# Attention, mixture of experts and a dense layer on one core: routing steps moved to another place on VectorE, an output tile put into the values' bank, and the end of the attention laid out anew

## Chip, core and metric

The kernel runs on one core of one Trainium2 chip. The metric is the device time in microseconds of one execution. Before the change it is 894.07 us, the median of 3 runs (893.64 to 894.19).

## What is computed

The reference chains three layers, all in float32:

```python
scores = q @ k.T / sqrt(64) + cum[:, None] - cum[None, :]   # cum: running sum of log f; causal
attn   = softmax(scores) @ v                                # 4 batches x 8 heads x 576 x 64
x      = attn, heads side by side                           # 2304 tokens x 512
logits = x @ w_gate + modality_bias[modality_id]            # 8 experts
e      = argmax(logits);  gate = softmax(logits)[e]
x      = gate * (relu(x @ w1[e]) @ w2[e])                   # w1: 512 x 1024, w2: 1024 x 512
h      = x @ w_in;  out = max(0.01 * h, h) @ w_out          # 512 -> 2048 -> 512
```

## The kernel before

**Attention (0 to 208 us).** Two heads make a group `g`; there are 16 groups, four to a batch. Each group goes through `first` (scores of query blocks 0 and 1), `last` (scores of block 4), `third` (block 2) and `fourth` (block 3). In these functions the group before is finished at the same time: `tr` transposes its probabilities on PE into PSUM tiles `pt_c`, ACT copies them to `tt`, `pv` multiplies them with the values in two parts (`pv_0`, `pv_1`, written to the one buffer of the pool `psv`), DVE copies the parts to `xu` and `xub`, and `xout` multiplies each with the identity beside the gate's weights (`xo_0`, `xo_1`). From `xo` DVE reads four times: `x` and `lp` of either part. `pt` and `xo` tiles rotate through the buffers of one pool, `pst`, so a transpose can be written only when DVE has read an `xo` tile of some time before. DVE also takes the maxima of the scores (`nm`) and prepares the operands of later groups (`raw`, `aq`).

**Routing.** `route(b)` is a generator of small steps for batch `b`: logits, the maximum `mx`, the one-hot `oh` of the chosen expert, ranks `rk` by matmul, and in the last step `lall`, five comparisons on DVE. `route1` makes the table of the first four expert slots by a matmul `tp` over `lall`, computes the row numbers from it on POOL and gathers the tokens of slots 0 and 1 (`xg`). Steps alternate between DVE, POOL, ACT and PE. `routed()` takes the next step of the oldest generator, whatever it is; it is called at fixed places of a group, and so a step lands where the count falls:

```python
        def routed(n=1):
            for _ in range(n):
                if routing and next(routing[0], 1):
                    routing.pop(0)
```

**Drain (208 to 224 us).** After the last group its tail remains: two `pt` tiles, `pv` and `xo`. The work of `drain` is put between that of slot 0's first matmul: `trx` transposes the gathered tokens (`tx`), `part0(k)` splits block `k` of the weights into a high part (ACT, `w1h`) and a low part (DVE, `w1l`), and starts the load of slot 1's weights. `gemm1` then makes `h` from three products a block, `keep` applies the activation on ACT (`hs`).

**Expert slots (to 470 us).** Slots of up to 128 tokens of one expert follow (`step`). Slots 1 to 3 split their weights only where the expert is another than that of the slot before: ACT and DVE read the word `nb` and branch (`tc.If` in `split`). In these inputs the branches aren't taken. The last batch's routing goes on in these steps; its places are the table `side`, as are those of `finish`, which makes the table of all further slots.

**Dense layer (480 to 890 us).** It is bound by PE and is not touched.

Work of each engine goes out in the order in which the code issues it; within some stretches (`ordered`) a scheduler keeps the order only for the engines that are named.

Of the kernel before, what the change touches and what calls it, by code (L numbers as in the profile page):

```python
# [74 lines left out]
def fused(ctx: ExitStack, tc, qk0, qk2, vp, f, mid, wg, mb, w1, w2, w_in, w_out, out):  # L75
# [93 lines left out]

    def parts(which, k):  # L170
        raw, hi, lo = (w2r, WL["2h"], WL["2l"]) if which else (w1r, w1h, WL["1l"])
        nc.scalar.copy(hi[k], raw[k])  # L172
        nc.vector.tensor_tensor(lo[k], raw[k], hi[k].bitcast(F32), ALU.subtract)  # L173
# [25 lines left out]
    with tc.tile_pool(name="pst", bufs=PST, space=PSUM) as pst:  # L199
# [277 lines left out]
        def pv(g, part):  # L477
            vt = vts[g]
            w = (XA, XB)[part]
            pv_ = psv.tile([P, 512], F32, tag="v", name=f"pv{g}_{part}")  # L480
            blocks = [(0, 0), (1, P), (2, 2 * P)] if part == 0 else [(0, 0), (1, 0), (2, 0), (3, 0), (4, P)]
            sb = st.pop((g, part))
            for b, q0 in blocks:
                for j in range(2):
                    nc.tensor.matmul(pv_[64 * j:64 * j + 64, q0:w], lhsT=vt[:, j, b, :], rhs=sb[:, j, b, q0:w], start=(b == 0), stop=(b == blocks[-1][0]))
            if part == 0:
                xu = a2.tile([P, w], F32, tag="xu", name=f"xu{g}")
            else:
                xu = xub
            st[g, "x", part] = xu  # L490
            nc.vector.tensor_copy(xu[:, :w], pv_[:, :w])

        def xout(g):
# [10 lines left out]
            for part, c0, n in ((0, 0, 3), (1, 3, 2)):  # L504
                xu = st.pop((g, "x", part))
                ps = pst.tile([P, 512], F32, tag="t", name=f"xo{g}_{part}")
                for i in range(n):
                    nc.tensor.matmul(ps[:, i * HW:(i + 1) * HW], lhsT=xu[:, i * P:(i + 1) * P], rhs=idw[:, gg, :], start=True, stop=True)
                i0 = ps[:, :n * HW].rearrange("p (c d) -> p c d", d=HW)
                sc = rr[:, c0:c0 + n, :].unsqueeze(3)  # L510
                for o, a, w in ((x[:, c0:c0 + n, gg * P:(gg + 1) * P], slice(0, P), D), (lp[:, c0:c0 + n, gg, :], slice(P, HW), E)):
                    nc.vector.tensor_tensor(o.rearrange("p c (j d) -> p c j d", j=2), i0[:, :, a].rearrange("p c (j d) -> p c j d", j=2), sc.to_broadcast([P, n, 2, w]), ALU.mult)
            if gg == H // 2 - 1:
                routing.append(route(b))
                if b == B - 1:
                    t0 = b * S
                    nc.sync.dma_start(xs[t0:t0 + 4 * P, :DM].rearrange("(c p) d -> p c d", p=P), x[:, 0:4, :DM])
                    nc.sync.dma_start(xs[t0 + 4 * P:t0 + S, :DM], x[:64, 4, :DM])
                if b == B - 2:
                    routing.append(route1(pre, (B - 1) * NC))  # L520
# [4 lines left out]

        RP = [pst, "t"]
# [22 lines left out]
        def route(b):  # L549
# [31 lines left out]
            rk = RP[0].tile([P, 512], F32, tag=RP[1], name=f"rk{b}")  # L581
            nc.tensor.matmul(rk[:, 0:4 * E], lhsT=before, rhs=oh[:, 0:4, :], start=True, stop=False)
            nc.tensor.matmul(rk[:, 4 * E:5 * E], lhsT=before[:64, :], rhs=oh[:64, 4, :], start=False, stop=False)
            nc.tensor.matmul(rk[:, 5 * E:6 * E], lhsT=onesb[:64, :], rhs=oh[:64, 4, :], start=False, stop=False)
            for c in range(4):
                nn = NC - c
                nc.tensor.matmul(rk[:, (c + 1) * E:6 * E].rearrange("p (c e) -> p c e", e=E), lhsT=onesb, rhs=oh[:, c, :].unsqueeze(1).to_broadcast([P, nn, E]), start=False, stop=(c == 3))
# [3 lines left out]
            if b < B - 1:  # L591
                nc.vector.reciprocal(x[:, :, DM], gs)
                for c in ((0, 2), (2, 4), (4, 5)) if b < B - 2 else ((0, 4), (4, 5)):
                    stores.append((b, x, *c))
            else:
                nc.vector.reciprocal(gs, gs)
                t0 = b * S
                nc.sync.dma_start(xs[t0:t0 + 4 * P, DM:].rearrange("(c p) d -> p c d", p=P), gs[:, 0:4].unsqueeze(2))
                nc.sync.dma_start(xs[t0 + 4 * P:t0 + S, DM:], gs[:64, 4:5])
# [11 lines left out]
            yield  # L611
            for c in range(NC):
                r = rows_of(c)
                nc.vector.tensor_scalar(lall[:r, b * NC + c, :], col[:r], pq[:r, c:c + 1], None, ALU.is_equal)

# [11 lines left out]
        def scan(a, n):  # L627
            t = [rt.tile([P, 4 + E], F32, name=f"scan{n}{i}") for i in range(2)]
            for i in t:
                nc.gpsimd.memset(i, 0.0)  # L630
            nc.gpsimd.tensor_copy(t[0][:, 4:], a)
            for s in (1, 2, 4):
                nc.gpsimd.tensor_add(t[1][:, 4:], t[0][:, 4:], t[0][:, 4 - s:4 + E - s])
                t = t[::-1]
            inc = t[0][:, 4:]
            exc = rt.tile([P, E], F32, name=f"exc{n}")
            nc.gpsimd.tensor_sub(exc, inc, a)
            return inc, exc
# [44 lines left out]
        def route1(tp, m):  # L683
# [9 lines left out]
            yield  # L693
# [19 lines left out]
            yield  # L713
            next(tb)
            yield
# [8 lines left out]
        routing = []  # L724

        def routed(n=1):
            for _ in range(n):
                if routing and next(routing[0], 1):
                    routing.pop(0)


        def first(g):
# [4 lines left out]
            store(1 + (g > 12))  # L737
            routed()
            if g == NG - 1:
                for w in range(2):  # L740
                    for k in range(4):
                        wload(0, w, k)
            for c in cs:
                c()
            for _ in then or ():
                pass

        def last(g):
            then = qk4(g) if g < NG else None
            if g:  # L750
                tr(g - 1, 4, (0, 1))
                routed()
# [4 lines left out]
        def third(g):  # L757
            then = qk(g, 2) if g < NG else None
            if g:
                routed()  # L760
# [7 lines left out]
        def fourth(g):  # L768
# [10 lines left out]
            routed()  # L779
# [5 lines left out]
        def finish_routes():  # L785
            while routing:
                if next(routing[0], 1):
                    routing.pop(0)
# [20 lines left out]
        def part0(k):  # L809
            parts(0, k)  # L810
            wload(1, 0, k)

        with ordered(tc, MS):
            prep_hi(1)
            for g in range(NG):
# [15 lines left out]
                if g:  # L831
# [3 lines left out]
                    routed()  # L835
                third(g)
                if not g:
                    last(g)
                fourth(g)
                routed()  # L840
# [86 lines left out]
    with tc.tile_pool(name="rt2", reuse_waits="tile", bufs=1) as rt2, \  # L927
# [17 lines left out]
        def split(t, which, k):  # L945
            if not 0 < t < K1:
                parts(which, k)
                if t + 1 < NS:
                    wload(t + 1, which, k)
            elif k == 3:  # L950

                if not WD:
                    WD.append(nc.values_load(nb[0:1, 0:1], engines=(mybir.EngineType.Activation, mybir.EngineType.DVE), min_val=0, max_val=2 ** K1 - 1))
                with tc.If(((WD[0] >> t) & 1) != 0):
                    for i in range(4):
                        parts(which, i)
                for i in range(4):
                    wload(t + 1, which, i)

        WD = []  # L960
# [54 lines left out]
        def step(t):  # L1015
            nx = t + 1 < NS
            if not t:
                split(t, 1, 0)
                split(t, 1, 1)
            keepg(t)  # L1020
            if t == K1 - 1:
                next(fini)
            if t + 2 < NS and t + 2 != K1:
# [3 lines left out]
            aside(t, "load")  # L1027
            if 0 < t < TE:
# [21 lines left out]
            if nx:  # L1050
# [22 lines left out]
        def finish():  # L1073
# [6 lines left out]
            tiles_of(nsl, cnt, P - 1)  # L1080
            nc.gpsimd.tensor_sub(nsl, nsl, used)
            inc, exc = scan(nsl, 2)
            nc.gpsimd.tensor_scalar(nt, inc[:, E - 1:E], float(K1), None, ALU.add)
            nc.gpsimd.tensor_sub(exc, exc, used)
# [49 lines left out]
        RP[:] = pmx, "tx"  # L1134
        fini = finish()
        late = routing.pop(0)
        for k, w in (((0, "b"), late), ((0, "d"), late), ((0, "d"), late), ((1, "load"), late), ((1, "a1"), late), ((1, "b"), fini), ((1, "pool"), late), ((1, "d"), late), ((1, "d"), fini), ((2, "load"), fini), ((2, "b"), fini)):
# [150 lines left out]
```

## Time and profile before

| what | value |
|---|---|
| median of 3 runs | 894.07 us (893.64 to 894.19) |
| profiled execution, its time | 891.73 us |
| profiled execution, its span | 890.0 us |
| TensorE clock granted, mean over the span | 0.991 of full speed |
| PE busy | 854.0 us, 96% of the span |

The span is that from the first to the last instruction of the profiled execution; its time is 1.7 us longer. The profiled execution is 2.3 us below the median of the three timed runs. All rows of the trace are of this one execution. A releaser named behind `<-` in a row is the instruction whose semaphore came last; `ACTq` and `DVEq` are the engines' sequencers, which run branches and loads of registers.

### The profile page before, as it was taken

The page shows a single profiled execution, that of the slowest core. Times are in us where ns is not written, and L with a number is a line of the kernel's source. Part 1 is how long each engine was busy: PE and PEld are TensorE (multiplying, and loading weights), DVE is VectorE, ACT ScalarE, POOL GpSimd, SP SyncE. Part 2 cuts the span into 40 slices and gives each one's busy share as a digit, 9 for nine tenths or more (in the row PEclk, how much of TensorE's full clock was granted, in tenths as well). Part 3 has the DMA queues.
Part 4 walks back from the last instruction along what each step waited for, and adds up shares of the span by engine and source line. Part 5 has one row for each costly group of instructions (what it writes and reads, how often), then busy time and mean ns, then how long its engine had stood idle before and what let it go on. Part 6 is the DMA issues. An engine that isn't in the chain of part 4 may idle for free. (4 is left out here: it accounts for less than half of the span.)

```text
span 890.0 us, 14390 instructions
## 1 busy us (share of the span) xinstructions
PE 854.0 (96%) x4733; PEld 707.6 (80%) x4733; DVE 583.8 (66%) x952; ACT 505.6 (57%) x969; POOL 194.3 (22%) x342
## 2 busy tenths in 40 slices
PE   5999999998899999999999999999999999999996
PEld 3788778886678888888787788888888888888885
DVE  6677677774558999999985373387337943473333
ACT  5787777875348999999984353453223422242221
POOL 5003122251737344544441000000000000001112
PEclk9999999999999999999999999999999999999998
DMA  5776776775268245121322240032001300011111
GB/s 152 206 183 190 207 206 179 201 178 198 78 205 301 69 153 168 55 70 41 115 96 60 64 143 13 1 99 91 0 1 48 119 25 0 1 48 48 48 48 72
DMA packets 33604, 92.93 MB, mean 104 GB/s; under 512 B 7957, under 2 KB 8629, under 8 KB 33522
## 3 DMA queue, kind: packets, MB, share of 16 engines
q1 hardware_dynamic: 28690, 76.70, 29.9%
q0 software_dynamic: 4800, 15.23, 5.0%
q8 instruction: 39, 0.64, 0.3%
q14 instruction: 43, 0.35, 0.1%
q10 hardware_dynamic: 32, 0.01, 0.0%
HBM read 132.09 MB, written 14.99 MB: 165 GB/s over the span
## 5 line engine op out<-in xcount | busy, mean ns | idle before, releaser
L1180 ACT COPY us<-u 128x512 f32<-128x512 f32 (+1 forms) x80 | 43.5, 544 | 163.7 <-PE u L1178 163.6
L1181 DVE SCALAR_TENSOR_TENSOR us<-u,us 128x512 f32<-128x512 f32 (+1 forms) x80 | 51.0, 637 | 125.8 <-ACT us L1180 125.2
L1178 PE MATMUL u<-fxl,whii 128*128 128x512 f32 (+1 forms) x320 | 118.1, 369 | 0.0
L1178 PE MATMUL u<-fxh,wloi 128*128 128x512 f32 (+1 forms) x320 | 117.9, 369 | 0.0
L1178 PE MATMUL u<-fxh,whii 128*128 128x512 f32 (+1 forms) x320 | 116.9, 369 | 0.7 <-ACT fxh L878 0.7
L1198 PE MATMUL a<-whio,gh 128*128 128x512 f32 x280 | 109.7, 392 | 0.0
L1198 PE MATMUL a<-wloo,gh 128*128 128x512 f32 x280 | 109.2, 390 | 0.0
L1198 PE MATMUL a<-whio,gl 128*128 128x512 f32 x280 | 103.2, 390 | 0.0
L173 DVE TENSOR_TENSOR w1l<-w1r,w1h 128x1024 fp32r<-128x1024 f32 x72 | 87.0, 1226 | 11.7 <-ACT w1h L172 11.4
L1208 POOL DMA_INDIRECT out<-acc,tid x18 | 17.7, 983 | 326.4 <-DVE acc L1205 272.0
L173 DVE TENSOR_TENSOR w2l<-w2r,w2h 128x1024 fp32r<-128x1024 f32 x68 | 80.7, 1227 | 1.2 <-ACT w2h L172 1.0
L399 ACT ACTIVATE p<-sc,nm 128x128 f32<-128x128 f32 (+3 forms) x128 | 66.0, 524 | 25.2 <-DVE nm L394 23.0
L1183 ACT CAST gh<-us 128x512 fp32r<-128x512 f32 (+1 forms) x76 | 44.6, 587 | 57.8 <-DVE us L1181 38.1
L172 ACT CAST w1h<-w1r 128x1024 fp32r<-128x1024 f32 x72 | 73.8, 1053 | 1.6 <-PE h L190 1.5
L1184 DVE TENSOR_TENSOR gl<-us,gh 128x512 fp32r<-128x512 f32 (+1 forms) x76 | 49.3, 648 | 38.3 <-ACT gh L1183 37.4
L394 DVE TENSOR_REDUCE nm<-sc 128x2 f32<-128x256 f32 (+1 forms) x64 | 51.0, 818 | 30.1 <-PE sc L390 26.6
L172 ACT CAST w2h<-w2r 128x1024 fp32r<-128x1024 f32 x68 | 69.3, 1050 | 2.4 <-PE y L983 1.3
L1178 PEld LDWEIGHTS u<-fxh,whii 128*128 128x128 f32 x320 | 60.2, 188 | 11.1 <-ACT fxh L878 0.9
L1178 PEld LDWEIGHTS u<-fxl,whii 128*128 128x128 f32 x320 | 60.3, 188 | 10.3
L1178 PEld LDWEIGHTS u<-fxh,wloi 128*128 128x128 f32 x320 | 60.3, 188 | 10.3
L983 PE MATMUL y<-w2h,hh 128*128 128x512 f32 x160 | 65.0, 406 | 0.0
L983 PE MATMUL y<-w2h,hl 128*128 128x512 f32 x160 | 62.9, 393 | 0.0
(296 smaller groups left out, 1858.4 us busy)
## 6 DMA issues: line engine op xcount, KB each, us to landing
w1r<-w SPq DMA_DIRECT2D x88, 512.0 KB
w2r<-w SPq DMA_DIRECT2D x82, 512.0 KB
rwi<-w_in SPq DMA_DIRECT2D x16, 512.0 KB
rwo<-w_out SPq DMA_DIRECT2D x16, 512.0 KB
raw<-qk SPq DMA_DIRECT2D x14, 576.0 KB
vt<-vp SPq DMA_DIRECT2D x16, 320.0 KB
xr<-yd SPq DMA_DIRECT2D x18, 256.5 KB
bk<-aq SPq DMA_DIRECT2D x15, 288.0 KB
```

Source lines behind the costliest of these rows:

```text
L172: nc.scalar.copy(hi[k], raw[k])
L173: nc.vector.tensor_tensor(lo[k], raw[k], hi[k].bitcast(F32), ALU.subtract)
L394: nc.vector.tensor_reduce(nm, view, axis=AX.X, op=ALU.max, negate=True)
L399: st["exp"] = nc.scalar.activation(pt[:, j, :], view[:, j, :], AF.Exp, bias=nm[:, j:j + 1], scale=1.0, accum_out=sms[g % 3][:, c, j:j + 1])
L983: nc.tensor.matmul(Yp[t], lhsT=ap[:, k * P:(k + 1) * P], rhs=wp[k // 2][:, k % 2, :], start=(k == 0 and i == 0), stop=(k == NFB - 1 and i ...
L1178: nc.tensor.matmul(ps, lhsT=w[:, c], rhs=x[:, k, :], start=(k == 0 and i == 0), stop=(k == NKB - 1 and i == 2))
L1180: nc.scalar.copy(us, ps)
L1181: nc.vector.scalar_tensor_tensor(us, ps, 0.01, us, ALU.mult, ALU.max)
L1183: nc.scalar.copy(gh, us)
L1184: nc.vector.tensor_sub(gl, us, gh.bitcast(F32))
L1198: nc.tensor.matmul(A[b][i], lhsT=x[:, c], rhs=w, start=(first and m == 0), stop=(last and m == 2))
L1208: d = nc.gpsimd.indirect_dma_start(out=out[:, :], out_offset=bass.IndirectOffsetOnAxis(ap=tid[:, c:c + 1], axis=0), in_=Y[b, i], in_offset ...
```

## The change

Four things change.

1. Routing steps have named places. A table `plan` maps a place in a group (`first`, `last`, `third`, `idle`, `end`, `after`) to the batch whose next step goes there. The place `idle` is new: it stands between the copy `xub` and the maximum of block 3's scores. One small multiplication (`eq` with `rev`) goes from POOL to DVE.
2. For groups up to 13, `xo_1` has no tile of `pst` any more. It is written to columns 192 to 479 of the bank in which `pv_1` of the same group stood in columns 0 to 191.
3. `drain` is written in another order, and `part0` is taken apart into `high` (ACT) and `low` (DVE). `high(0, 0)` goes up into the last group. The loads of slot 1's weights stand together behind the splits.
4. The branch of slot 1 (`split(1, 0, 3)`) is issued directly after `keep(0)`. The last batch has a generator of its own, `late_route`, wholly on DVE except for its matmul and its exponential; `side` has other places for it and for `finish`, whose scan moves from POOL to DVE. The fourth slot's table matmul is issued after `gemm1` of slot 3 has begun, and its gather behind that.

```diff
+                st[g, "half"] = pv_
...
-                ps = pst.tile([P, 512], F32, tag="t", name=f"xo{g}_{part}")
+                ps = st.pop((g, "half"))[:, XB:] if part and g < NG - 2 else pst.tile([P, 512], F32, tag="t", name=f"xo{g}_{part}")
...
-                routing.append(route(b))
+                routing[b] = (route if b < B - 1 else late_route)(b)
...
-            nc.gpsimd.tensor_tensor(eq, eq, rev.unsqueeze(1).to_broadcast(shp), ALU.mult)
-            yield
+            nc.vector.tensor_tensor(eq, eq, rev.unsqueeze(1).to_broadcast(shp), ALU.mult)
...
+        def late_route(b):
...
+            mx, eq, m2, lm = t1("mx"), t3("eq"), t1("m2"), t3("lm")
+            nc.vector.tensor_reduce(L, lp, axis=AX.X, op=ALU.add)
+            nc.vector.tensor_add(L, L, bia[:, b * NC:(b + 1) * NC])
+            nc.vector.tensor_reduce(mx, L, axis=AX.X, op=ALU.max)
+            nc.vector.tensor_tensor(eq, L, mx.unsqueeze(2).to_broadcast(shp), ALU.is_equal)
+            nc.vector.tensor_tensor(eq, eq, rev.unsqueeze(1).to_broadcast(shp), ALU.mult)
+            nc.vector.tensor_reduce(m2, eq, axis=AX.X, op=ALU.max)
+            nc.vector.tensor_tensor(oh, eq, m2.unsqueeze(2).to_broadcast(shp), ALU.is_equal)
+            st["late"] = nc.vector.tensor_tensor(lm, L, mx.unsqueeze(2).to_broadcast(shp), ALU.subtract)
+            yield
...
+            if b < B - 2:
+                places += [(a, "end"), (a + 1, "third"), (a + 1, "idle"), (a + 2, "idle")]
...
         def drain(g):
+            for k in range(4):
+                wload(0, 1, k)
+            pv(g, 0)
+            low(0, 0)
             tr(g, 4, (0, 1))
+            high(0, 1)
+            cs = [tr(g, 3, (j, )) for j in range(2)]
+            for c in cs:
+                c()
+            low(0, 1)
             trx(0, pst, "t")
-            pv(g, 0)
-            part0(0)
-            for c in [tr(g, 3, (j, )) for j in range(2)]:
-                c()
+            high(0, 2)
+            pv(g, 1)
+            low(0, 2)
+            high(0, 3)
             gemm1(0, 0, 1, psc, "sc")
-            part0(1)
-            pv(g, 1)
             trx(1, pst, "t")
+            low(0, 3)
             gemm1(0, 1, 2, psc, "sc")
-            part0(2)
+            for k in range(4):
+                wload(1, 0, k)
             xout(g)
-            part0(3)
             gemm1(0, 2, 4, psc, "sc")
             keep(0)
-            next(routing[0])
+            split(1, 0, 3)
+            next(routing[B - 1])
...
             if not t:
-                split(t, 1, 0)
-                split(t, 1, 1)
+                with tc.issue_after(st["late"].ins):
+                    split(t, 1, 0)
+                    split(t, 1, 1)
             keepg(t)
-            if t == K1 - 1:
-                next(fini)
-            if t + 2 < NS and t + 2 != K1:
+            if t + 2 < NS and t + 2 not in (K1, K1 + 1):
                 gather(t + 2)
...
-            if nx:
+            if nx and t:
                 split(t + 1, 0, 3)
...
-        for k, w in (((0, "b"), late), ((0, "d"), late), ((0, "d"), late), ((1, "load"), late), ((1, "a1"), late), ((1, "b"), fini), ((1, "pool"), late), ((1, "d"), late), ((1, "d"), fini), ((2, "load"), fini), ((2, "b"), fini)):
+        for k, w in (((1, "load"), late), ((1, "b"), late), ((1, "pool"), late), ((1, "pool"), late), ((1, "d"), fini), ((1, "d"), fini), ((2, "load"), late), ((2, "load"), fini), ((2, "d"), fini), ((3, "load"), fini)):
```

How the order of instructions moves is shown at three places. Names end in a number that tells tiles of one name apart.

The first place is DVE in the group in which batch 0's routing ends with `lall`. Before:

```order
L394 TENSOR_REDUCE nm_0_1222<-sc_01_1211 128x2
L394 TENSOR_REDUCE nm_1_1224<-sc_01_1211 128x2
L366 SCALAR_TENSOR_TENSOR raw_969<-raw_969,qs,aq_1156 128x1152
L614 TENSOR_SCALAR lall<-col,pq_1189 128x128 x4
L614 TENSOR_SCALAR lall<-col,pq_1189 64x128
L441 TENSOR_REDUCE nm_4_1257<-sc_4_1256 128x1
L491 COPY xu_1284<-pv_0_1277 128x384
L394 TENSOR_REDUCE nm_2_1294<-sc_2_1287 128x2
L491 COPY xub<-pv_1_1296 128x192
L394 TENSOR_REDUCE nm_3_1329<-sc_3_1322 128x2
```

The same step of the same batch in the changed kernel:

```order
L421 TENSOR_REDUCE nm_0_1371<-sc_01_1360 128x2
L421 TENSOR_REDUCE nm_1_1373<-sc_01_1360 128x2
L393 SCALAR_TENSOR_TENSOR raw_1134<-raw_1134,qs,aq_1324 128x1152
L468 TENSOR_REDUCE nm_4_1401<-sc_4_1400 128x1
L519 COPY xu_1428<-pv_0_1421 128x384
L421 TENSOR_REDUCE nm_2_1438<-sc_2_1431 128x2
L519 COPY xub<-pv_1_1440 128x192
L626 TENSOR_SCALAR lall<-col,pq_1308 128x128 x4
L626 TENSOR_SCALAR lall<-col,pq_1308 64x128
L421 TENSOR_REDUCE nm_3_1478<-sc_3_1471 128x2
```

`lall` stood ahead of `nm_4` and of the copy `xu` of `pv_0`; it now stands behind the copy `xub`, ahead of `nm_3`.

The second place is PE at the beginning of the drain, behind the last `xo`. Before:

```order
L463 MATMUL pt_4_0_2954<-ident,p_176 128x128 x3
L463 MATMUL pt_4_3_2959<-ident,p_176 128x128 x2
L178 MATMUL tx_2963<-ident,xg_131 128x128 x4
L485 MATMUL pv_0_2970<-tt_0_2902,vt_2723 64x384 x2
L485 MATMUL pv_0_2970<-tt_0_2902,vt_2723 64x256 x2
L485 MATMUL pv_0_2970<-tt_0_2902,vt_2723 64x128 x2
L473 MATMUL pt_3_0_3000<-ident,p_3_2950 128x128 x4
L473 MATMUL pt_3_1_3005<-ident,p_3_2950 128x128 x4
L190 MATMUL h_3012<-w1h_133,xh_137 128x512 x2
L190 MATMUL h_3012<-w1h_133,xl_138 128x512 x2
L190 MATMUL h_3012<-w1l_2607,xh_137 128x512 x2
L485 MATMUL pv_1_3022<-tt_1_2953,vt_2723 64x192 x8
```

After:

```order
L512 MATMUL pv_0_2940<-tt_0_2884,vt_2719 64x384 x2
L512 MATMUL pv_0_2940<-tt_0_2884,vt_2719 64x256 x2
L512 MATMUL pv_0_2940<-tt_0_2884,vt_2719 64x128 x2
L490 MATMUL pt_4_0_2951<-ident,p_176 128x128 x3
L490 MATMUL pt_4_3_2956<-ident,p_176 128x128 x2
L500 MATMUL pt_3_0_2961<-ident,p_3_2933 128x128 x4
L500 MATMUL pt_3_1_2966<-ident,p_3_2933 128x128 x4
L205 MATMUL tx_2974<-ident,xg_131 128x128 x4
L512 MATMUL pv_1_2982<-tt_1_2950,vt_2719 64x192 x8
L512 MATMUL pv_1_2982<-tt_1_2950,vt_2719 64x64 x2
L217 MATMUL h_2996<-w1h_133,xh_137 128x512 x2
L217 MATMUL h_2996<-w1h_133,xl_138 128x512 x2
```

`pv_0` goes from behind `tx` (the first gathered tokens) to the front, and `pt_3` goes ahead of `tx` too; `pv_1` now follows `tx` directly and stands ahead of the first `h`.

The third place is DVE at the end of slot 0's splits, around slot 1's branch (`TENSOR_LOAD nb` to the second branch; the four `w1l` between stand inside it). Before:

```order
L173 TENSOR_TENSOR w1l_2610<-w1r_126,w1h_136 128x1024
L173 TENSOR_TENSOR w2l_3152<-w2r_127,w2h_3148 128x1024
L173 TENSOR_TENSOR w2l_3153<-w2r_128,w2h_3149 128x1024
L530 TENSOR_REDUCE mx_3172<-lgs 128x5
L567 TENSOR_TENSOR eq_3174<-lgs,mx_3172 128x40
L953 TENSOR_LOAD nb
L954 REGISTER_ALU x2
L954 COMPARE_AND_BRANCH
L173 TENSOR_TENSOR w1l_2607<-w1r_123,w1h_133 128x1024
L173 TENSOR_TENSOR w1l_2608<-w1r_124,w1h_134 128x1024
L173 TENSOR_TENSOR w1l_2609<-w1r_125,w1h_135 128x1024
L173 TENSOR_TENSOR w1l_2610<-w1r_126,w1h_136 128x1024
```

After:

```order
L540 TENSOR_TENSOR lp_189<-xo_1_3049,rr_3039 128x2x16
L193 TENSOR_LOAD nb
L194 REGISTER_ALU x2
L194 COMPARE_AND_BRANCH
L179 TENSOR_TENSOR w1l_2618<-w1r_123,w1h_133 128x1024
L179 TENSOR_TENSOR w1l_2619<-w1r_124,w1h_134 128x1024
L179 TENSOR_TENSOR w1l_2620<-w1r_125,w1h_135 128x1024
L179 TENSOR_TENSOR w1l_2621<-w1r_126,w1h_136 128x1024
L194 UNCONDITIONAL_BRANCH x2
L650 TENSOR_REDUCE lgs<-lp_189 128x40
L651 TENSOR_TENSOR lgs<-lgs,bia 128x40
L652 TENSOR_REDUCE mx_3119<-lgs 128x5
```

Two `w2l` splits and the last batch's `mx` and `eq` stood ahead of the branch; the branch now follows the last read of `xo` (`lp`), and the logits, summed on DVE (`lgs`), come behind it.

## Rows read from the trace of the kernel before

**Rows 1.** The page, part 1: engine, busy us, share of the span, instructions.

```profile
PE 854.0 (96%) x4733; PEld 707.6 (80%) x4733; DVE 583.8 (66%) x952; ACT 505.6 (57%) x969; POOL 194.3 (22%) x342
```

**Rows 2.** Windows: us; per engine busy (x instructions); granted clock; DMA share; GB/s.

```profile
30.00:196.00 166.00, 160.86 (x1361) 134.02 (x1357) 119.87 (x261) 130.47 (x367) 37.73 (x125) 1.00 0.72 188
...
208.00:232.00 24.00, 18.03 (x102) 12.49 (x100) 13.87 (x27) 12.38 (x21) 6.43 (x11) 0.93 0.42 149
...
266.00:443.00 177.00, 177.00 (x859) 146.35 (x860) 170.20 (x190) 161.19 (x213) 82.28 (x59) 1.00 0.38 124
```

**Rows 3.** Waits of PE from 25 to 208 us: total us, times, longest.

```profile
PE pt L473 <- DVE lp L512: 2.4, 8, 0.8
PE pv L485 <- DVE xu L491: 2.0, 3, 0.7
PE xo L508 <- ACT tt L475: 0.7, 3, 0.2
```

**Rows 4.** Timeline of DVE, 186 to 198 us: start, duration, work [idle before <-releaser].

```profile
188.29 0.92 DVE L614 TENSOR_SCALAR lall<-col,pq 128x128 bf16<-128x128 bf16 x5 [0.73 <-POOL pq L547]
...
189.77 0.54 DVE L491 COPY xu<-pv 128x384 f32<-128x384 f32 x1
...
194.07 1.22 DVE L394 TENSOR_REDUCE nm<-sc 128x2 f32<-128x1024 f32 x1 [1.54 <-PE sc L390]
...
197.11 0.18 DVE L512 TENSOR_TENSOR lp<-xo,rr 128x32 f32<-128x32 f32 x1
```

**Rows 5.** Timeline of PE, 196 to 208 us.

```profile
199.39 0.95 PE L671 MATMUL tp<-h,lall 128*128 128x8 bf16 x15
200.27 1.52 PE L485 MATMUL pv<-tt,vt 128*64 128x384 f32 x12
```

**Rows 6.** Timeline of PE, 206 to 231 us, the drain.

```profile
207.98 0.49 PE L463 MATMUL pt<-ident,p 128*128 128x128 f32 x3
209.14 0.41 PE L463 MATMUL pt<-ident,p 128*128 128x128 f32 x2 [0.67 <-DVE lp L512]
211.30 0.74 PE L178 MATMUL tx<-ident,xg 128*128 128x128 f32 x4 [1.75 <-DMA xg<-xs,gidx]
...
214.73 1.25 PE L473 MATMUL pt<-ident,p 128*128 128x128 f32 x8
...
225.40 0.73 PE L190 MATMUL h<-w1l,xh 128*128 128x512 f32 x2 [0.93 <-DVE w1l L173]
227.29 0.73 PE L190 MATMUL h<-w1h,xh 128*128 128x512 f32 x2 [1.16 <-ACTq L954]
...
229.96 0.73 PE L190 MATMUL h<-w1l,xh 128*128 128x512 f32 x2 [1.47 <-DVEq L954]
```

**Rows 7.** Windows of 2 us in the drain, columns as in the second group.

```profile
212.00:214.00 2.00, 2.00 (x9) 0.98 (x10) 0.69 (x1) 1.53 (x2) 0.00 (x0) 0.50 0.75 295
```

**Rows 8.** Timeline of ACT, 203 to 231 us.

```profile
212.56 1.05 ACT L172 CAST w1h<-w1r 128x1024 fp32r<-128x1024 f32 x1
215.58 1.07 ACT L475 COPY tt<-pt 128x512 f32<-128x512 f32 x2 [1.98 <-PE pt L473]
...
226.17 1.02 ACT L195 ACTIVATE hs<-h 128x1024 f32<-128x1024 f32 x1 [2.13 <-PE h L190]
```

**Rows 9.** Timeline of DVE, 205 to 231 us.

```profile
225.26 2.84 DVE L173 TENSOR_TENSOR w2l<-w2r,w2h 128x1024 fp32r<-128x1024 f32 x2
228.61 0.20 DVE L530 TENSOR_REDUCE mx<-lgs 128x5 f32<-128x40 f32 x1 [0.51 <-POOL lgs L561]
```

**Rows 10.** Timeline of DVE, 252 to 262 us.

```profile
255.69 0.20 DVE L674 COPY tq<-tp 128x42 f32<-128x42 f32 x1 [2.67 <-PE tp L671]
```

**Rows 11.** Timeline of POOL, 255 to 264 us.

```profile
257.15 1.00 POOL L994 DMA_INDIRECT yd<-ys,oidx  x1 [1.25 <-ACT gc L963]
258.17 1.10 POOL L546 TENSOR_SCALAR idt<-tq 128x21 f32<-128x21 f32 x1
```

**Rows 12.** Timeline of PE, 264 to 268 us.

```profile
265.90 0.66 PE L178 MATMUL tx<-ident,xg 128*128 128x128 f32 x4 [0.88 <-DMA xg<-xs,gidx]
```

More of the change, by code (lines that the diff above doesn't have):

```diff
@@ L519, in xout @@
                 if b == B - 2:
-                    routing.append(route1(pre, (B - 1) * NC))
+                    routing[B] = route1(pre, (B - 1) * NC)
         lps = [pre.tile([P, NC, H // 2, 2 * E], F32, name=f"lp{i}") for i in range(2)]
@@ L580, in route @@
             yield
[L581 to L587, printed above, removed]
+            rk = ranks(b, oh, pst, "t")
             yield
@@ L614, in route, with ranks @@
                 nc.vector.tensor_scalar(lall[:r, b * NC + c, :], col[:r], pq[:r, c:c + 1], None, ALU.is_equal)
+        def ranks(b, oh, pool, tag):
+            rk = pool.tile([P, 512], F32, tag=tag, name=f"rk{b}")
+            nc.tensor.matmul(rk[:, 0:4 * E], lhsT=before, rhs=oh[:, 0:4, :], start=True, stop=False)
+            nc.tensor.matmul(rk[:, 4 * E:5 * E], lhsT=before[:64, :], rhs=oh[:64, 4, :], start=False, stop=False)
+            nc.tensor.matmul(rk[:, 5 * E:6 * E], lhsT=onesb[:64, :], rhs=oh[:64, 4, :], start=False, stop=False)
+            for c in range(4):
+                nn = NC - c
+                nc.tensor.matmul(rk[:, (c + 1) * E:6 * E].rearrange("p (c e) -> p c e", e=E), lhsT=onesb, rhs=oh[:, c, :].unsqueeze(1).to_broadcast([P, nn, E]), start=False, stop=(c == 3))
+            return rk
@@ L723, in fused, with routed @@
             start()
[L724 to L729, printed above, removed]
+        routing = {}
+        plan = {}
+        for b in range(B - 1):
+            a = 4 * b + 5
+            places = [(a - 1, "end"), (a, "idle" if b < B - 2 else "first")]
+            if b < B - 2:
+                places += [(a, "end"), (a + 1, "third"), (a + 1, "idle"), (a + 2, "idle")]
+            else:
+                places += [(a, "last"), (a, "third"), (a, "idle"), (a + 2, "first")]
+            for k in places:
+                plan.setdefault(k, []).append(b)
+        for k in ((13, "end"), (14, "idle"), (14, "idle"), (15, "last"), (15, "after")):
+            plan.setdefault(k, []).append(B)
+        def routed(g, at):
+            for b in plan.get((g, at), ()):
+                next(routing[b], 0)
         def first(g):
@@ L736, in first @@
                 prep_lo(g + 1)
[L737 to L742, printed above, removed]
             for c in cs:
                 c()
+            store(1 + (g > 12))
+            routed(g, "first")
+            if g == NG - 1:
+                for k in range(4):
+                    wload(0, 0, k)
             for _ in then or ():
@@ L751, in last @@
                 tr(g - 1, 4, (0, 1))
-                routed()
+                routed(g, "last")
                 pv(g - 1, 0)
@@ L778, in fourth @@
                 c()
-            routed()
+            routed(g, "fourth")
             if g:
@@ L838, in fused @@
                     last(g)
+                if g == NG - 1:
+                    high(0, 0)
+                routed(g, "idle")
                 fourth(g)
-                routed()
+                routed(g, "end")
             drain(NG - 1)
@@ L943, in fused @@
         oc = mw.tile([P, 2], I32, name="oc")
[L945 to L960, printed above, removed]
         def keepg(t):
@@ L1027, in step @@
             aside(t, "load")
+            if t + 2 == K1 + 1:
+                gather(t + 2)
             if 0 < t < TE:
```

115 lines of the change are left out of this document (77 added, 38 removed).

## The prediction

> **What bounds the kernel now.** I read the page's busy times first: PE works 96% of the span [rows 1], so the kernel is as long as PE's work and PE's gaps, and only a gap, or work done at the lower clock, can be won. Next, windows by stage [rows 2]. From 266 to 443 us, the expert slots, PE is busy all 177.00 of 177.00 us: there is nothing to win there, and VectorE with 170.20 us has little room. The dense layer is not touched. In the attention, 30 to 196 us, PE idles 5.1 us of 166; in the drain, 208 to 232 us, 6.0 us of 24, and its granted clock there is only 0.93. These two stretches are what the change rearranges, so I looked at every gap in them.
>
> In the attention the list of waits has three kinds [rows 3]: a transpose `pt` waits for DVE's read `lp` of an old `xo` (eight times, 2.4 us), `pv_1` for the copy `xu` (three times, 2.0), `xo` for ACT's copy `tt` (three times, 0.7). Together 5.1 us, all the idle time of that stretch. DVE's timeline shows where the second kind comes from [rows 4]: DVE waits 0.73 us for POOL's `pq`, does five `lall` in 0.92, then the maximum of block 4, and reaches `xu` only at 189.77. Before the maximum of block 3 it then idles for 1.54 us, waiting for scores. That is the hole into which `lall` goes.
>
> In the drain PE's timeline has these waits [rows 6]: 0.67 for `lp` (209.14), 1.75 for the gathered `xg` (211.30), 0.93 for a late `w1l` (225.40), 1.16 for ACT behind the activation `hs` (227.29), and 1.47 for DVE's branch (229.96): 5.98 us.
>
> **The drain, part by part.** The clock: in 212 to 214 us the granted clock is 0.50 [rows 7], the lower of the two levels, 1.2 GHz, and the stretch follows the 1.75 us in which PE stood for `xg`. Over the 24 us of the stretch 0.93 of the clock means 0.07 x 24 = 1.7 us lost [rows 2]. [...]
>
> With `pv_0` first, `lp` has 1.52 us [rows 5] instead of none to be read: the 0.67 goes. `tx` then comes behind `pv_0` (1.52), the five `pt_4` transposes (about 0.9, by their two rows at 207.98 and 209.14) and eight `pt_3` (1.25): 207.98 + 1.5 + 0.9 + 1.25 = 211.6, while PE could start on `xg` at 211.30 in the old run [rows 6]. The cover is thin, 0.3 us, and the table `tp` (0.95) now goes behind `pv_0` of group 14 instead of ahead, which makes the gather later by up to 1.5. If the whole of this arrives, 1.2 us of wait are back and the clock may fall; I take the wait as gone, with that as a rival. The other splits now run ahead of need: `high(0, 0)` moves into the last group, each `w1h` costs ACT 1.05 [rows 8], and ACT had 1.98 us idle ahead of the `pt_3` copies [rows 8]; so the 0.93 for `w1l` goes. DVE's branch stood behind two `w2l` (2.84 us) and `mx`, which waited 0.51 for POOL's logits [rows 9]; now it stands behind the last `lp`, so the 1.47 goes.
>
> What stays or comes new. `hs` needs all of `h`, takes 1.02 us from 226.17 on [rows 8], and slot 1's first `h` started right behind it, at 227.29 [rows 6]: the 1.16 stays, under either bound (0 if ACT were ahead, 2.2 if the two more `w2h`, now issued ahead of `hs`, are still running). New is a wait of `pv_1`: it needs ACT's copies of `pt_4` and of `pt_3` (1.07 for two) [rows 8], and `w1h_1` (1.05) is issued between them, while PE has only `pt_3` and `tx` (0.7) to do in that time. ACT's first `pt_4` copy can start when its transposes end, some 2.1 us behind the last `xo`; 0.7 for the copies (by the 1.07 for eight blocks, five of them), 1.05, 1.07 bring it to 5.1. PE is there at 1.5 + 0.9 + 1.25 + 0.5 = 4.0 or so. I take 1.2 (bounds 0, where `w1h_1` slips behind, and 2.3, both splits ahead). Drain: 5.98 + 1.7 - 1.16 - 1.2 = 5.3 us less.
>
> The late routing on DVE: eight small operations at 0.20 [rows 9] stand ahead of four `w2l`, where POOL had done part of it. DVE's work is later by about 1.6 us there, but `w2l` is used only in slot 0's second matmul, a whole `gemm1` of slot 1 later; I cost it at nothing. Were that cover gone it would cost those 1.6 us.
>
> **The attention, part by part.** `xo_1` in the values' bank takes one tile of ten out of the pool's rotation, so the transposes that waited for `lp` get another, longer-free buffer: the 2.4 us go. With `lall` in the hole, 0.92 of its 1.54 us, `xu` is earlier by 0.73 + 0.92 = 1.65, far more than the waits of 0.65: 2.0 us go. The 0.7 us for `tt` came in the same three groups, behind the same delay: they go too (bounds 0 and 0.7). What comes back: batch 2 keeps its `lall` ahead of the maximum of block 4, in the last group, without the wait for POOL but with two operations of the table behind it, and five operations of 0.20 stand ahead of the same maximum in group 13. Its old wait was 0.65, of which 0.73 of DVE's wait is gone and 0.6 of operations come; I take 0.5 given back (0 to 1.3). Sum: 5.1 - 0.5 = 4.6 us less.
>
> **The fourth slot's table.** Its matmul is issued behind twelve matmuls of `gemm1`. Before, DVE copied it at 255.69 [rows 10], but POOL turned to it only at 258.17, because it waited 1.25 for ACT's `gc` and sent a `yd` of 1.00 first [rows 11]; PE then waited 0.88 for the gather [rows 12]. A table later by 2.8 us ends at 258.5 instead of 255.7, about 0.3 to 0.5 behind what POOL gave it before. I take +0.5 (bounds -0.88, all of that wait, and +2.8).
>
> **Sum.** -4.6 - 5.3 + 0.5 = -9.4 us against the profiled execution's 891.73 (span 890.0): 882.3. The median of the runs lies 2.3 above that execution; 894.07 - 9.4 = 884.7.
>
> **The rivals.** (a) `xg` late in the drain: the thin cover fails, PE stands 1.2 us or more before `tx`, and the clock falls as before. That gives back 1.2 to 3.3 us (wait and 1.7 of clock, with the rest of the chain): 886 to 888. For it: the DMA queues are what `xg` waited for, and the clock did fall there [rows 6, 7]. Against: 2.4 us more of work stand ahead of `tx`.
> (b) Only the drain gains: in the attention the wait removed is replaced by the next one behind it, ACT's copies `tt` above all, since ACT is 130.47 us busy of 166 [rows 2] and already ends some waits [rows 3]. Then -5.3 + 0.5: 889.3.
> (c) More than forecast: `pv_1` and `hs` find ACT ahead, and the fourth table costs nothing: 2.4 to 3 us more, 881.7 to 882.3.
> (d) The change doesn't do what it says: waits only move; 894.
> (e) Slower: the values' bank. `psv` has one buffer, and `pv_0` of the next group now waits until DVE has read `xo_1` out of it. DVE's last `lp` ends at 197.3 [rows 4], `pv_0` could start without `tp` at 199.39 [rows 5]: a slack of 2.1 us in each of 13 groups. A read later by 2.1 us costs nothing; each further us costs 13. The gain of 9.4 and the 1.8 of the bound below are gone at (9.4 + 1.8) / 13 = 0.86 us beyond the slack, where the time is 895.9. Against it: DVE idles in each group [rows 4]. By the Trainium skill, "PSUM — Partial Sum Buffer", section "PSUM bank collisions raise a hardware error", PE's writes and DVE's reads of one bank have to be kept apart by bank, not by address, so the two halves serialize; no run here shows what it costs.
>
> **How the numbers follow.** Forecast 0.50 (its own range 882.7 to 886.7: the bounds of `pv_1`, `hs` and the table), (a) 0.20, (b) 0.12, (c) 0.07, (d) 0.06, (e) 0.05. The range 881.5 to 890.0 takes in all but (d) and (e). A measurement tells about 0.2%, 1.8 us, from no change: faster 0.89, same 0.06, slower 0.05.
>
> **What would show it.** In the changed kernel's profile: no wait of `pt` for `lp` and none of `pv` for `xu` between 25 and 208 us; `lall` in batch 0 and 1 behind `xub`; the clock 1.00 through the drain; one wait of about 1.2 us before `pv_1`, one before slot 1's `h`, no `DVEq`; at slot 4's `tx` 0.9 to 1.5 us. The prediction is wrong if a wait of `pv_0` for DVE appears in many groups, if PE stands for `xg` in the drain, or if ACT is named where DVE was.

## The result, and the profile after

The changed kernel takes 880.7 us, the median of 4 runs (880.36 to 884.77), against 893.86 (890.74 to 894.19) for the kernel before: ratio 0.9871, 95% interval 0.9834 to 0.9907. The interval is wide because the runs of the two kernels lie 3.5 and 4.4 us apart, which is part of the story. Forecast were 884.7 us and a ratio of 0.9895. The ratio compares the means of the runs, and 0.9871 of the 894.07 shown before is 882.5; the medians alone stand at 0.9853. One of the executions below, of the kernel with the bank only, took 1068.18 us at a mean granted clock of 0.756; it is a slow one and is left out of all comparisons.

The page of the changed kernel, its busy times and the granted clock in 40 slices:

```profile
PE 847.2 (96%) x4733; PEld 703.6 (80%) x4733; DVE 588.2 (67%) x981; ACT 503.3 (57%) x969; POOL 182.0 (21%) x305
...
PEclk9999999999999999999999999999999999999998
```

PE is busy 847.2 us instead of 854.0 [rows 1] for the same 4733 matmuls. The work is the same, so some of it ran faster. The row of the clock doesn't show it: a slice is 22 us long, and the page of the kernel before has the same row. Windows by stage (columns as in the group of before):

```profile
30.00:191.00 161.00, 159.57 (x1364) 134.35 (x1362) 120.81 (x262) 129.77 (x369) 37.78 (x129) 1.00 0.76 195
...
203.00:222.00 19.00, 16.33 (x109) 13.22 (x106) 15.45 (x29) 11.19 (x17) 2.26 (x3) 1.00 0.57 168
...
256.00:432.00 176.00, 176.00 (x855) 145.47 (x854) 169.34 (x189) 160.33 (x212) 82.09 (x59) 1.00 0.38 120
```

In the attention PE idles 1.4 us of 161 instead of 5.1 of 166; in the drain 2.7 of 19 at clock 1.00 instead of 6.0 of 24 at 0.93 [rows 2]. The expert slots have no gap, as before. PE's waits from 25 to 203 us, total us, times, longest:

```profile
PE sc L411 <- ACT p L426: 1.0, 3, 0.3
PE sc L411 <- DMA aq<-aq: 0.6, 2, 0.3
PE pt L490 <- ACT tt L502: 0.3, 1, 0.3
```

None of the three kinds of [rows 3] is left, no `pv` waits for a read of the values' bank, and new small waits for operands have come: 1.9 us in all. The drain on PE's timeline:

```profile
201.92 1.51 PE L512 MATMUL pv<-tt,vt 128*64 128x384 f32 x12
...
203.97 1.23 PE L500 MATMUL pt<-ident,p 128*128 128x128 f32 x8
206.03 0.63 PE L205 MATMUL tx<-ident,xg 128*128 128x128 f32 x4 [0.84 <-DMA xg<-xs,gidx]
206.59 1.77 PE L512 MATMUL pv<-tt,vt 128*64 128x192 f32 x20
...
217.61 0.73 PE L217 MATMUL h<-w1h,xh 128*128 128x512 f32 x2 [1.83 <-ACTq L194]
```

`pv_0` now covers the read of `lp`, but the gathered rows are late by 0.84 us all the same. `pv_1` follows `tx` without a wait, and slot 1's first `h` waits 1.83 instead of 1.16 [rows 6]. ACT's and POOL's timelines tell why:

```profile
205.59 1.08 ACT L502 COPY tt<-pt 128x512 f32<-128x512 f32 x2
...
215.81 1.02 ACT L222 ACTIVATE hs<-h 128x1024 f32<-128x1024 f32 x1 [0.82 <-PE h L217]
```

```profile
197.80 1.34 POOL L168 DMA_INDIRECT xg<-xs,gidx  x1 [1.02 <-DMA w1r<-w]
```

The `pt_3` copies end at 206.67, when `pv_1` has just begun, so the wait for `xg` hid the one that I expected at `pv_1`. `hs` ends at 216.83, but `h` starts only at 217.61. The gather goes out at 197.80 and its rows are there at 205.9, 3.9 us behind the last `xo`, where it was 3.0 before (211.2 and 208.2). It wasn't sent later: it went out 4.2 us ahead of the end of that `xo`, and 3.8 ahead of it in the kernel before:

```profile
204.36 1.34 POOL L168 DMA_INDIRECT xg<-xs,gidx  x1 [0.96 <-DMA w1r<-w]
```

From issue to landing it took 8.1 us instead of 6.8; with `tx` put first (below) it is 6.7 at most. No run here shows why. At slot 4's `tx` PE waits 2.21 us instead of 0.88 [rows 12]:

```profile
255.74 0.66 PE L205 MATMUL tx<-ident,xg 128*128 128x128 f32 x4 [2.21 <-DMA xg<-xs,gidx]
```

I divided every profile of this study at four points of PE's timeline: the first `pv`, the end of the last `xo` of the 15th group, the first `th` (slot 0's result), and the first `y` of slot 4. In us, with the falls of the clock below 0.9 ahead of the span's last 10 us:

| kernel | to first `pv` | attention | drain | slots 0 to 4 | span | falls of the clock, us |
|---|---|---|---|---|---|---|
| before | 28.98 | 179.17 | 24.15 | 55.61 | 890.0 | 24 to 28, 212 to 216, 470 to 476 |
| before, again | 27.92 | 179.91 | 22.62 | 56.48 | 887.8 | none |
| changed | 27.72 | 174.27 | 18.87 | 56.96 | 878.7 | none |
| changed, again | 28.47 | 175.72 | 20.36 | 56.68 | 882.1 | 22 to 28, 220 to 226 |
| changed, third | 29.07 | 174.04 | 18.90 | 56.57 | 879.4 | none |

The first row less the third: 1.26 + 4.90 + 5.28 - 1.35 = 10.1, and 1.2 more behind these stretches, where only the first has the fall at 470 to 476: the 11.3 of the spans. The forecast had 0 + 4.6 + 5.3 - 0.5.

The last row lists no fall, but its start ran at the lower level all the same: a transpose `pt` of 128x128 takes 421 ns in it up to 27 us and 273 from 28 us on, and 421 is also what it takes in the fall at 25 us of the first row. The granted clock reads 1.00 there, since its first entry in this profile is at 27.6 us. So the start's 29.07 us are the clock's doing too, and a mean clock can hide a microsecond or more there.

### The profile page after: what moved, and what is told of

Its sections match the earlier page's. It is cut to its first block, busy times and chain, and to the rows that moved or that the text cites. A ratio compares the mean times of both kernels' runs of the same rounds, so it can differ in the third digit from the quotient of the medians.

```text
span 878.7 us, 14400 instructions
## 1 busy us (share of the span) xinstructions
PE 847.2 (96%) x4733; PEld 703.6 (80%) x4733; DVE 588.2 (67%) x981; ACT 503.3 (57%) x969; POOL 182.0 (21%) x305
```

## Experiments

### How much is the clock, and is it the change's?

The two kernels were run again, unaltered.

> The changed kernel unaltered. Of its 11.3 us of shorter span 2.5 lie where nothing was rearranged: 1.3 in the start (20 to 30 us, granted clock 0.83 before, 1.00 after) and 1.2 ahead of the dense layer (470 to 476 us, 0.50 before, 1.00 after). Theory: these two falls of the clock come and go from execution to execution and are no part of the change; then this profile shows one of them in some executions, and the times of one kernel lie up to 2.5 us apart. Rival: the change keeps the clock up by the shorter waits; then the clock is 1.00 at both places here again, and the fastest time is again 880.4.

> The kernel before, unaltered. Theory (clock by chance): at least one of the two falls, in the start or ahead of the dense layer, is missing in this profile, and its span is shorter than 890.0 us by 1.2 to 2.5. Rival (clock by the kernel): both falls stand where they stood, span 890.0 within 0.3. The drain's fall behind the wait for the gathered rows is expected in either case.

> The changed kernel once more, unaltered, as a yardstick on the same chip for the two beside it, and for how often its clock falls. Theory: executions without a fall before the dense layer's end take 880.3 to 880.6, those with one or two 882 to 885; a fall is rarer than in the kernel before, whose median lies 4 us above its own fastest. Rival: as often as before, median 884 or more.

The kernel before now took 889.46 us (890.74 was the best of its earlier runs), span 887.8, and no fall anywhere before 880 us. That goes further than I had expected: I had put down the drain's fall as certain, and PE waited there for `xg` as long as before. PE's row and windows of the kernel before, again:

```profile
210.93 0.63 PE L178 MATMUL tx<-ident,xg 128*128 128x128 f32 x4 [1.70 <-DMA xg<-xs,gidx]
```

```profile
208.00:212.00 4.00, 1.64 (x12) 0.96 (x12) 1.10 (x4) 1.89 (x6) 0.00 (x0) 1.00 1.02 413
212.00:216.00 4.00, 4.00 (x33) 2.72 (x29) 2.71 (x4) 3.15 (x5) 0.00 (x0) 1.00 0.16 57
```

In 208 to 212 PE works 1.64 us of 4, and the clock stays at 1.00; in the first profile of the same code it stood at 0.50 behind the same wait [rows 7]. The changed kernel in turn had falls in its second profile, 883.8 us, one of them behind the wait for slot 1:

```profile
218.00:220.00 2.00, 0.14 (x1) 0.14 (x2) 1.83 (x8) 1.02 (x1) 0.73 (x2) 1.00 1.02 394
...
222.00:224.00 2.00, 2.00 (x6) 1.28 (x4) 1.93 (x2) 0.00 (x0) 0.00 (x0) 0.50 0.98 152
```

So a fall follows a wait, but the same wait doesn't always bring one. One place shows it best: in all thirteen profiles of this study PE waits 1.9 us for a `th` ahead of the dense layer (at 470.6 us in the first), and the clock falls behind it in three of them. That holds for the term "1.7 us of clock" of my sum too: it is a matter of how often. Over the 13 runs that were timed together here, with their mean clocks, the kernel before took 889.4 us at a clock of 0.995 to 0.997 (2 of 13) and 892.7 to 895.6 at 0.989 to 0.992 (10 of 13); one run had 892.4 at 0.995. The changed kernel took 880.4 to 882.6 at 0.994 to 0.998 in 10 runs of 12 and 883.8 and 884.8 at 0.993 in the other two; its medians in three sets of runs are 880.7, 882.61 and 881.95. None of the third set took the 880.3 to 880.6 that I had expected of a run without a fall; its profiled run, with none listed, took 881.12, and reached its first `pv` 1.35 us later than the first profile of the changed kernel. Both theories hold in part: the falls come and go, and the changed kernel has fewer. Its fastest run is 9.0 below the fastest of the kernel before (880.36 against 889.36), the medians lie 11 to 13 apart; by the mean clocks, the difference is falls that the kernel before has in most executions.

### The values' bank, added and taken away

> The kernel before with one edit: the second output tile in the values' bank. Theory: the eight waits of transposes for lp (2.4 us) go and nothing comes in their place; the last output tile ends 2.4 us earlier (205.7), and the whole is 2.4 us faster at an equal clock. Rival: the next wait takes their place (ACT's copies, or the values' bank held by DVE so that the next group's first values product waits): gain under 0.5, or a loss with pv waiting for DVE's x or lp in many groups.

```diff
 kernel before
+                st[g, "half"] = pv_
-                ps = pst.tile([P, 512], F32, tag="t", name=f"xo{g}_{part}")
+                ps = st.pop((g, "half"))[:, XB:] if part and g < NG - 2 else pst.tile([P, 512], F32, tag="t", name=f"xo{g}_{part}")
```

> The changed kernel with the second output tile in the rotation of the transposes' pool again, nothing else. Theory: the gain of the bank stands by itself: the waits of transposes for lp come back, 0.2 each in about eight groups and up to 0.8 in one, and the attention, 174.3 to 175.9 us from the first values product to the last output tile in six profiles, takes 2.2 to 2.4 longer, 176.6 to 178.2. Rival: with routing out of DVE's way lp is read in time anyway, the attention stays under 176.

```diff
 changed kernel
-  ... if part and g < NG - 2 else pst.tile(...)
+  ... if part and g < 0 else pst.tile(...)
```

Bank only: 889.88 us, the median of nine runs (886.54 to 893.83), ratio 0.9968 (0.9943 to 0.9992) to the kernel before. PE's waits in its attention:

```profile
PE pv L485 <- DVE xu L492: 2.0, 3, 0.7
PE xo L509 <- ACT tt L475: 0.7, 3, 0.2
PE sc L384 <- ACT p L399: 0.7, 2, 0.3
```

The eight waits for `lp` are gone, the waits for `xu` and `tt` stand as in [rows 3], and no `pv` waits for a read of the bank. The attention takes 177.33 us, 1.8 to 2.6 less than in the two profiles before; the medians lie further apart (893.72 less 889.88 is 3.8), and what the rest is isn't shown. Without the bank the changed kernel takes 883.98 us against 881.95 beside it, its attention 177.85, 2.0 to 3.8 more than in eight profiles of kernels with its bank and its places of `lall` (174.04 to 175.85), and the waits are back:

```profile
PE pt L500 <- DVE lp L540: 2.7, 9, 0.8
```

Both say the same: 2 to 3 us, and the rival of the held bank is out. The list of waits shows less than the whole. Between these two `pv_0` of the kernel before no gap is listed at all:

```profile
53.37 1.52 PE L485 MATMUL pv<-tt,vt 128*64 128x384 f32 x12
...
65.23 1.08 PE L485 MATMUL pv<-tt,vt 128*64 128x384 f32 x6
```

```profile
63.65 1.52 PE L512 MATMUL pv<-tt,vt 128*64 128x384 f32 x12
...
75.12 1.08 PE L512 MATMUL pv<-tt,vt 128*64 128x384 f32 x6
```

From start to start it is 11.86 us before and 11.47 in the changed kernel. Laid against each other, instruction by instruction, the two groups part by 0.17 at `xo` and by 0.18 at a `pt`. They are not the same group of the two kernels. The one that matches the second, from 65.23 us on in the kernel before, has one listed wait of 0.22 us and takes 11.88; it parts from the second by 0.38 at that one `pt`. So the list gave 0.22 us of 0.38 there. The likely reason is that the ends of matmuls are modelled, so that a short wait lies under the end of the matmul before; no run separates the two.

### The idle place

> The changed kernel with the comparisons lall of batches 0 and 1 taken out of DVE's idle place and put ahead of block 4's maximum again, with their input made a group earlier as in the changed kernel. Theory (the place matters): pv waits for xu again in two groups, 0.65 each, and xo for tt 0.24 each, 1.3 to 1.8 us slower up to the last output tile. Rival (the wait for POOL matters): the 0.73 us in which DVE waited for pq do not come back, xu is in time, and the cost is 0 to 0.2.

```diff
-                places += [..., (a + 1, "idle"), (a + 2, "idle")]
+                places += [..., (a + 1, "idle"), (a + 2, "first")]
```

```profile
PE pv L512 <- DVE xu L519: 1.2, 3, 0.6
```

Three waits for `xu`: 0.55 at 101 us and 0.23 at 150 in the two groups with the moved `lall`, and 0.38 at 174, which the changed kernel has as well (0.10 there). So 0.8 us of the 1.3 come back; the waits of `xo` for `tt` don't. The attention is 176.13, just above the eight (174.04 to 175.85), the median 882.44. It stands between the two theories: by the waits, the idle place carries about half, and the rest would be the earlier `pq`, which no run takes back. The times can't tell it from nothing.

### PE's order in the drain

> The changed kernel with PE's order at the drain's beginning put back: the last transposes and the gathered tokens' transposes first, the values products and pt_3 behind them. The gathered rows land about 4 us behind the last output tile whatever PE does. Theory: PE waits some 0.7 us for lp and 2.5 for the rows instead of 0.84 in all, so the drain is 2.4 us longer at full clock, and the long wait brings falls of the clock in the drain in most executions (granted clock 0.989 to 0.993 over the span, as the kernel before has): median 884 to 886. Rival (falls by chance, order without weight because pv_1 then finds its copies ready): drain longer by less than 1 us, clock of most runs 0.996 and more, median 881 to 883.

```diff
         def drain(g):
+            tr(g, 4, (0, 1))
+            trx(0, pst, "t")
             pv(g, 0)
             low(0, 0)
-            tr(g, 4, (0, 1))
             high(0, 1)
...
-            trx(0, pst, "t")
```

885.93 us (884.21 to 887.36, 5 runs), ratio 0.9894 (0.9875 to 0.9914). Waits of PE, 200 to 225 us, and two windows:

```profile
PE h L217 <- ACTq L194: 1.9, 1, 1.9
PE tx L205 <- DMA xg<-xs,gidx: 1.0, 1, 1.0
PE pt L490 <- DVE lp L540: 0.7, 1, 0.7
PE pv L512 <- ACT tt L502: 0.2, 1, 0.2
```

```profile
208.00:212.00 4.00, 3.76 (x22) 2.26 (x18) 2.52 (x4) 1.91 (x4) 0.00 (x0) 0.67 0.08 30
...
222.00:230.00 8.00, 6.96 (x33) 5.46 (x34) 6.04 (x10) 1.45 (x4) 0.00 (x0) 0.79 0.78 160
```

The size of the waits I had wrong: they are 0.67 + 1.05 + 0.24 = 1.96 against 0.84, so 1.1 more, not 2.4, since here the rows landed 2.3 us behind the last `xo`. But the drain takes 23.46 instead of 18.87: the clock fell twice in it, to 0.67 and 0.79 in these windows, behind the wait for `xg` and behind that for slot 1. The slowest run of the changed kernel but one, of twelve, is faster than the fastest of these five; at the median they differ by 3 to 5 us, of which waits are 1.1. So the order pays. That it pays by the clock is shown for the profiled execution alone, the slowest of the five, at a mean clock of 0.989. I had expected 0.989 to 0.993 in most; the other four ran at 0.995 and 0.996, as several runs of the changed kernel did, and took 884.21 to 886.37 all the same. What makes up the rest there is open.

### Slot 1's branch

> The changed kernel with the last batch's eight routing operations (2.2 us) ahead of slot 1's branch on DVE. Theory: ACT's branch, which ends 0.7 us behind hs, releases slot 1's first matmul at 217.6, and DVE's branch ends at about 217.2 even so; nothing is lost (0 to 0.3), and the place of the branch ahead of the chain is worth nothing here: what paid was that the w2l splits and POOL's logits no longer stand ahead of it. Rival (the forecast's view, the branch's place pays): 1.0 to 1.5 us slower, with a wait of w1l's matmul for DVE's branch.

```diff
-            split(1, 0, 3)
             next(routing[B - 1])
+            split(1, 0, 3)
```

882.44 us (880.36 to 883.24). DVE and PE:

```profile
217.15 0.19 DVE L657 TENSOR_TENSOR lm<-lgs,mx 128x40 f32<-128x40 f32 x1
218.89 3.50 DVE L179 TENSOR_TENSOR w2l<-w2r,w2h 128x1024 fp32r<-128x1024 f32 x3 [1.55 <-DVEq L194]
```

```profile
217.92 0.73 PE L217 MATMUL h<-w1h,xh 128*128 128x512 f32 x2 [1.83 <-ACTq L194]
...
218.96 0.69 PE L217 MATMUL h<-w1l,xh 128*128 128x512 f32 x2
```

DVE comes out of its branch only at 218.9, 1.55 us behind the chain, as the load of its word counts too. PE's `w1l` matmul starts at 218.96 without a wait, since PE stood for ACT until 217.92. The theory holds in its result, with little to spare (I had expected DVE's branch at 217.2): the branch ahead of the chain gains nothing here, as long as PE stands for ACT.

> The changed kernel with slot 1's branch on ACT ahead of the activation hs. Theory: of the 1.83 us in which slot 1's first matmul waits, 0.67 are the load of the branch's word, which stands between hs and the branch on ACT; they go, and 1.16 stay, because the matmul also needs hs to have read slot 0's result: 0.7 us faster. Rival 1: the matmul waits for the branch alone, not for hs: 1.6 faster. Rival 2: the wait is that of hs in full, no gain.

```diff
-            keep(0)
             split(1, 0, 3)
+            keep(0)
```

ACT and PE of this kernel:

```profile
217.46 1.02 ACT L222 ACTIVATE hs<-h 128x1024 f32<-128x1024 f32 x1 [0.48 <-PE h L217]
```

```profile
218.54 0.74 PE L217 MATMUL h<-w1h,xh 128*128 128x512 f32 x2 [1.11 <-ACT hs L222]
```

The wait falls from 1.83 to 1.11 and its releaser is now `hs` itself; the drain takes 18.18 instead of 18.87. That is the theory, to 0.03 us. The median of 882.71 (882.49 to 883.22) doesn't show it. This profile, at 882.85, has a fall at 256 to 262, behind the wait at slot 4; the other three runs, at mean clocks of 0.994 to 0.996, were not profiled.

### The fourth slot's table

> The changed kernel with the fourth slot's table matmul ahead of gemm1 of slot 3, as it stood before. Theory: the table's 2.8 us later place delays the gather, and the wait before slot 4's transposes (2.0 to 2.2 us in the three profiles of the changed order, 0.9 to 1.7 in three of the old one) falls to 0.5 to 1.2: 0.8 to 1.5 us faster. Rival: the gather's time on the DMA queues sets the wait, or the table's operands from DVE come too late for the early place and PE waits there instead: under 0.3 either way.

```diff
             keepg(t)
+            if t == K1 - 1:
+                next(fini)
...
-  ..., ((2, "d"), fini), ((3, "load"), fini)):
+  ..., ((2, "d"), fini)):
```

POOL in the changed kernel, and POOL and PE here:

```profile
244.56 1.01 POOL L1061 DMA_INDIRECT yd<-ys,oidx  x1 [7.66 <-ACT gc L1030]
247.32 1.19 POOL L572 TENSOR_SCALAR idt<-tq 128x21 f32<-128x21 f32 x1 [1.76 <-DVE tq L746]
```

```profile
245.81 1.01 POOL L1061 DMA_INDIRECT yd<-ys,oidx  x1 [7.55 <-ACT gc L1030]
246.83 0.33 POOL L572 TENSOR_SCALAR idt<-tq 128x21 f32<-128x21 f32 x1
```

```profile
244.53 1.37 PE L743 MATMUL tp<-h,lall 128*128 128x42 bf16 x20 [0.27 <-DVEq L194]
...
255.12 0.60 PE L205 MATMUL tx<-ident,xg 128*128 128x128 f32 x4
```

In the changed kernel POOL sends `yd` and then stands 1.76 us until the table is there; here the table is there when `yd` is out. The wait before slot 4's `tx` is gone altogether, more than I expected, for 0.27 us of PE ahead of `tp`. The stretch from slot 0's `th` to slot 4 takes 55.05 us instead of 56.96: 1.9 faster. Best run 879.49, median 880.51 (one of the four fell to 883.9 at clock 0.989).

### Both mends

> The changed kernel with both mends: slot 1's branch on ACT ahead of hs, and the fourth slot's table ahead of gemm1 of slot 3. Theory: they lie in different stretches and add up, 0.7 and 1.9 by the waits of their single runs: fastest 877.8 to 878.3, median 879 to 880.5, and faster than both kernels. Rival: with slot 1 earlier, the table's operands or the gather are late by as much, and only one of the two shows (fastest 878.6 to 879.7).

879.02 us (877.30 to 880.04, 5 runs), ratio 0.9830 (0.9814 to 0.9847) to the kernel before, where the changed kernel beside it had 881.95 (881.12 to 882.44) and 0.9867 (0.9851 to 0.9883). Drain 18.16, slots 0 to 4 55.01: the two mends add up, 2.9 us at the median, faster than both kernels. The fastest run lies below the 877.8 to 878.3 that I expected. The wait for slot 1:

```profile
PE h L217 <- ACT hs L222: 1.1, 1, 1.1
```

## Why the prediction was right, point by point

**The size, and luck in it.** The way and the stretches were right; the gain was larger than forecast. The median of 880.7 lies 4.0 us below 884.7, and below the range that I gave (881.5 to 890.0); only by the ratio of the means, 882.5, is the change inside it, and then next to rival (c) with its 881.7 to 882.3, of whose three conditions only the one on `pv_1` held. Of the 4.0 us, 1.9 lie in the profiled execution (a span of 878.7 against 880.6 by my sum). The rest is that I let the median lie 2.3 above the profiled execution, as in the kernel before, and in the changed kernel it lies 0.3 above. The forecast's own range of 2 us either way doesn't follow from the bounds it names: added up, those of `pv_1`, `hs` and the table go from 3.7 below the forecast to 4.4 above it.

By my own signs the mechanism was wrong in one place: PE does stand for `xg` in the drain. That the sum came out there was luck, as follows.

**Attention, -4.6.** Right: 179.2 and 179.9 became 174.0 to 175.9 in eight profiles, 4.7 at their mean of 174.9. The bank's 2.4 measured 2 to 3. The copies' 2.0 came; 0.8 of it was taken back by the place alone. The 0.5 given back is there at the named place, group 13: at 172 to 174 us `pv` waits for `xu`, 0.10 us in the first profile of the changed kernel (too short for the list) and up to 0.71 in others. Rival (b) happened on a small scale: waits of `sc` for ACT and for `aq`.

**Drain, -5.3.** The sum was right, 5.28 in the two first profiles, and its parts were not. At full clock the drain went from 22.62 to 18.9: 3.7, where the waits of my sum give 5.98 - 2.36 = 3.6. Of these, the `pv_1` term of 1.2 measured 0, the `xg` term of 0 measured 0.55 to 0.91 (rival (a), without its fall), and `hs` of 1.16 measured 1.83, because ACT loads the branch's word between `hs` and the branch: the bound of 2.2 took `w2h` for the danger, which were done. In the first profile the three errors are -1.2, +0.84 and +0.67, and nearly cancel. The `pv_1` term was also added up wrongly: 2.1 + 0.7 + 1.05 + 1.07 is 4.9, not 5.1, and PE's own 1.5 + 0.9 + 1.25 + 0.5 is 4.15, so it should have been 0.8. The cover for `xg` failed because the rows took 1.3 us longer to land, which I had not reckoned with; the later `tp`, which I had, sent them no later. The 0.93 for `w1l` is gone, though no run takes the earlier splits back by themselves. The 1.47 for the branch did go; that its place ahead of the chain did it, as I put it, was wrong. The other 1.5 us of the 5.28 are the fall in the first profile of the kernel before, which the next profile of it doesn't have.

**The clock, -1.7.** Not a term but a chance. I read one execution's fall as the kernel's price, and two other falls of that same execution, some 1.3 us each at 24 and 470 us, as nothing: with these gone from the first profile of the changed kernel the span is 2 us shorter than my sum. That a wait of this size brings a fall I took as a rule from that one execution; here a wait of 1.70 us passed without one. In the drains with the old order the clock fell five times in four profiles (before, twice; bank only; `tx` first), in those with the new order twice in nine.

**The table, +0.5.** The mechanism was right, the size was not: 0.9 at the mean of the profiles without a fall there (from 56.0 to 56.9), and 1.9 against the place tried above. I had costed the delay against POOL's `yd` alone; the table is 1.76 us behind even that.

**Rival (e)** did not show in any profile: no `pv` waits for a read of the bank in the changed kernel or with the bank alone, in any of the 14 groups that use it (my sum had 13).

## What to carry to other kernels

Profile a kernel more than once before a fall of the clock, or its absence, goes into a sum; in these profiles a wait of PE of a microsecond or two brought a fall at some times and not at others. An order that shortens waits seems to buy fewer falls, too. Before a branch on an engine, look at what its sequencer has to load first, and put the load and the branch ahead of the work that doesn't need them. A producer that moves behind twelve matmuls has to be costed to the one who waits for it last, here a gather and its matmul, not to the next engine.

## What was not expected of the hardware

PE's list of waits lacked 0.2 to 0.4 us in a group (11.86 and 11.88 us from start to start against 11.47, with 0 and 0.22 listed), so start-to-start times are the safer measure. The clock behind one and the same wait of 1.9 us fell in three profiles of thirteen. And the attention of one and the same code took 174.04 to 175.72 us in three profiles at full clock from 30 us on, with waits for DMA-fed operands (`aq`) that come and go, so differences of a microsecond there need several profiles.
